# Both halves of the PE array get their block of x from one transfer, half 1 one block ahead

## The chip, the core and the metric

The kernel runs on one core of a Trainium2 chip. The core's engines work side by side, each through its own list of instructions in order: PE (matrix multiply), DVE and ACT (element-wise work), POOL (element-wise work, and it can start transfers), and SP, which in this kernel only starts transfers (DMA) between DRAM and the on-chip memory. Semaphores order the engines among each other. The metric is the device time of one execution in microseconds (us); less is better. Three runs of the kernel before took 2618.78, 2620.35 and 2619.97 us, median 2619.97.

## The reference

The input x is 2048 tokens by D = 576. What is computed, in float32:

```python
xn = layernorm(x)
qkv = (xn @ wqkv).reshape(B, S, 3, H, Dh)      # 32 heads of 18
p = softmax(q @ k.T * Dh ** -0.5)               # per head, 2048 x 2048
s = (p @ v).reshape(B, S, D) @ wo
u = xn @ w_up                                   # 576 -> 4608
g = xn @ w_gate
b = (u * g) @ w_down                            # 4608 -> 576
out = x + s * silu(b)
```

## The kernel before, in words

**Stages.** A first stage (to about 195 us in the trace) normalizes x, turns it so that D lies on partitions, makes q, k and v, and stores them in DRAM. The main stage (195 to about 2545 us) runs attention and the gated linear unit (GLU) interleaved on PE. The last stage multiplies by `wo` and writes the output.

**Two halves of PE.** In the main stage most matmuls use 64 of the 128 rows of the array, so that one on rows 0 to 63 ("half 0") and one on rows 64 to 127 ("half 1") run at the same time. PE takes its list in order; a half starts its next matmul when that matmul's turn has come and the half is free. Half 0 makes the score matmuls whose maximum DVE takes (L651) and the up projections (L756); half 1 makes the score matmuls whose exponential ACT takes (L703) and the gate projections (L756); the down projections (L807) are split over both. The product of probabilities and v (L714) takes the whole array, in 64 "visits" of 32 matmuls (64 in the trace, where each runs in two passes), two for each head.

**x for the GLU.** The 2048 tokens make four chunks (`c`) of 512. A chunk's x is cut into 9 blocks of 64 rows of D, and each value is held as a high and a low part, so `xg` (two tiles, `xg[0]` and `xg[1]`, of 9 slots each) has 18 slots per half. `x_part(b, part)` gives the tile and slot of a block's part. A projection is 27 matmuls, three for each block: `TERMS` at L746. Both halves need all 9 blocks in their own 64 rows, so before the change each half has its own transfers: `x_block(c, b, r)` copies blocks from the DRAM store `sx` into the rows of half `r`, two blocks in one transfer (block 4, which straddles the two tiles, in two small ones). SP's queue carries those of half 0, POOL's queue those of half 1 (L462). There is one buffer: block `b` of the next chunk may overwrite block `b` only after its last use, which is in the last projections of a chunk (`q == NF2 - 1 and n % 2`, L962). `x_first` fills `xg` for chunk 0 straight from the chip's memory, `x_store` writes the other chunks to `sx`.

**Units and weights.** The 4608 columns are cut in 18 parts; a unit is one chunk with one part: two up and two gate projections and 48 down matmuls on each half. In chunk 0 the weights come raw from the inputs (`g_raw`, L146: `w_up` to rows 0 to 63, `w_gate` to rows 64 to 127), are split in high and low parts by ACT and POOL, and are kept in DRAM (`swg`, `swd`); later chunks load the split weights from there (L244 into `wgu`, L283 into `wd`, 1152 KB each).

**What sets the order.** From 195 us on the order of all instructions is made by a planner at build time (`order()`, L1256). It keeps a clock for each half of PE and each engine, with fixed costs, and puts the next matmul where its inputs are due: `there` holds when blocks of x are due, `can_go` (L1189) lets a projection of a new chunk start on a block only then, `moved(start, MB)` (L1024) is its estimate for a transfer on SP's queue, `engine("POOL", ...)` the one for POOL. `stack_turn` asks for the stacks of q and k of the next head (tiles `whole` and `turning`, L319), and `max_rows` for the rows of negated maxima (L689). The planner's clock sets only the order; what runs when is set by semaphores.

The boundaries between chunks, called first, second and third below, lie near 740, 1340 and 1930 us in the trace.

Of the kernel before, what the change touches and what calls it, by code (L numbers as in the profile page):

```python
# [20 lines left out]
FT = mybir.dt.float32  # L21
# [20 lines left out]
def kernel(  # L42
# [10 lines left out]
    nc = tc.nc  # L53
    _, S, D = x.shape
# [5 lines left out]
    NCH = S // 512  # L60
# [6 lines left out]
    dram = ctx.enter_context(tc.tile_pool(name="dram", bufs=1, space=bass.MemoryType.DRAM))  # L67
# [3 lines left out]
    psum = ctx.enter_context(tc.tile_pool(name="psum", bufs=1, space=PSUM))  # L71

    sqk = dram.tile([2, 2, D, S], FT, name="sqk")
    sx = dram.tile([NCH, 9, 64, 2, 512], FT, name="sx")
    swg = dram.tile([2 * NF2, 128, 18, 128], FT, name="swg")
    swd = dram.tile([NF2, 128, 2, 2, D], FT, name="swd")
    sv = dram.tile([S, H, DH + 1], FT, name="sv")
# [67 lines left out]

    def g_raw(f):  # L146
        raw = wpool.tile([128, 9, 128], FT, name="wraw", bufs=2)
        for r, m in enumerate((w_up, w_gate)):
            nc.sync.dma_start(raw[64 * r:64 * r + 64], m[:, 128 * f:128 * f + 128].rearrange("(b p) c -> p b c", p=64))
        return raw  # L150

    def d_raw(p):
# [15 lines left out]
    clk, free, split_at = [0.0, 0.0], {"DVE": 0.0, "ACT": 0.0, "POOL": 0.0}, {}  # L168
# [7 lines left out]
    def engine(eng, start, length):  # L176
        start = max(free[eng], start)
        free[eng] = start + max(length - HIDDEN[eng], 0.03)
        return start + length
# [44 lines left out]
    def g_load(n):  # L224
        if n < 2 * NF2:
            graw[n] = g_raw(n)
# [231 lines left out]
    def x_part(b, part):  # L458
        return divmod(2 * b + part, 9)

    def x_block(c, b, r):
        queue = nc.gpsimd if r else nc.sync  # L462
        if b == 4:
            for part in range(2):
                queue.dma_start(xg[part][r:r + 64, 8 - 8 * part, :].bitcast(FT), sx[c, b, :, part, :])
        elif b in (1, 3, 6, 8):
            i, k = x_part(b - 1, 0)
            queue.dma_start(xg[i][r:r + 64, k:k + 4, :].rearrange("p (b e) s -> p b e s", b=2).bitcast(FT),
                            sx[c, b - 1:b + 1].rearrange("b p e s -> p b e s"))

    vbox, vrows, vturn = {}, [], [0]

# [48 lines left out]
    def x_store(c, ks):  # L521
        for k in ks:
            src = xcs[c][:, k, :].bitcast(FT)
            if k < 8:
                nc.sync.dma_start(sx[c, 2 * (k % 4):2 * (k % 4) + 2, :, k // 4, :].rearrange("b p s -> (b p) s"), src)
            else:
                for part in range(2):
                    nc.sync.dma_start(sx[c, 8, :, part, :], src[64 * part:64 * part + 64])

    def x_first(b, part):  # L530

        i, k = x_part(b, part)
        j, r0 = (4 * part + b // 2, 64 * (b % 2)) if b < 8 else (8, 64 * part)
        for r in (0, 64):
            nc.sync.dma_start(xg[i][r:r + 64, k, :].bitcast(FT), xcs[0][r0:r0 + 64, j, :].bitcast(FT))  # L535

    raws = {}
# [60 lines left out]
    for t in range(8, NT):  # L598
# [4 lines left out]
        if t == 11:  # L603
            xg = [xcp.tile([128, 9, 512], FR, name="xc")]
# [28 lines left out]
    with ExitStack() as mid:  # L633
# [115 lines left out]
        def gu_start(r, n):  # L749
            ready(gdone, n)  # L750
            return bank("g", 1, slots[r, "g"])
# [45 lines left out]
        def alone(u, n):  # L797
            return u == len(units) - 1 and n == 7
# [148 lines left out]
            wos[1] = wpool.tile([128, 2, D], FR, name="wos2", tag="wgu", bufs=2)  # L947
            nc.sync.dma_start(wos[1].bitcast(FT), swo[:, 8:10, :])

        passed, xdone = {}, []  # L950

        def stream(r, kind):

            def glu(n):
                c, q = units[n // 2]
                box = []
                for k in range(len(TERMS)):
                    def work(k=k):
                        if k == 0:
                            box.append(gu_start(r, n))  # L960
                        gu_op(r, n, box[0], k)
                        if q == NF2 - 1 and n % 2 and k % 3 == 2 and c < NCH - 1:  # L962
                            b = k // 3
                            x_block(c + 1, b, 64 * r)
                            if b in (1, 3, 4, 6, 8):
                                if r:
                                    at = engine("POOL", clk[r] + 0.5, 0.75 + 0.6 * (b == 4)) + 3.0
                                else:
                                    at = moved(clk[r] + 0.5, 0.285 if b == 4 else 0.57)
                                for e in (b,) if b == 4 else (b - 1, b):  # L970
                                    there["x", c + 1, e, r] = at
                        if n == 2 * len(units) - 1 and k == 13:
                            xdone.append(r)
                            if len(xdone) == 2:
                                wo_fetch()
                        if k == len(TERMS) - 1:
                            highs.append((gate_end if r else up_end)(n, box[0]))
                    end = (("DVE", 0.685) if r else ("ACT", 0.595)) if k == len(TERMS) - 1 else None
                    yield 0.231, k == 0, work, end, ("g", n, k), len(TERMS)

            def down(u, n):
                own = alone(u, n)
                key = u, n, r * own
                s, i = divmod(n, 2)
                for k in range(len(DTERMS)):
                    def work(k=k):
                        if (own or r == 0) and k == 0:
                            passed[key] = down_start(r, u)
                        down_op(r, u, s, i, passed[key], k, {"POOL": nc.gpsimd, "ACT": nc.scalar, "DVE": nc.vector}[soonest()])
                        if (own or r) and k == len(DTERMS) - 1:  # L990
                            acts.append(by_act(u, i, clk[r] + 0.33))
                            down_end(u, s, i, passed.pop(key), acts[-1])
                    end = None
                    if (own or r) and k == len(DTERMS) - 1:
                        end = (None, 0.0)
                    yield 0.132, (own or r == 0) and k == 0, work, end, ("d", u, 6 * n + k), len(DTERMS)

            if kind == "g":
                for n in range(2 * len(units)):
                    yield from glu(n)  # L1000
            else:
                for u in range(len(units)):
                    for n in range(8):
                        yield from down(u, n)
# [19 lines left out]
        def moved(start, size):  # L1024

            queue[0] = max(queue[0], start) + size / 0.24
            return queue[0] + 2.0

        due, jobs, rows_done = [], [], {}
        there, queue = {}, [0.0]  # L1030
        na = nb = 0
        part_work = len(units) * (2 * 27 * 0.231 + 4 * 12 * 0.132)
        part = part_work + (TOTAL + N + LEAD) * 0.231
# [155 lines left out]
        def can_go(r, first, ev):  # L1189

            kind, n, k = ev
            now = clk[r]
# [10 lines left out]
            c, q = units[u]  # L1203
# [10 lines left out]
                if not r and n > 0 and low_end.get(n - 1, 1e9) > now + 0.4:  # L1214
                    return False
            if c and q == 0 and n % 2 == 0:
                return there.get(("x", c, k // 3, r), 1e9) <= now
            return True

        def late(goal, r=0):  # L1220
# [117 lines left out]
    with ExitStack() as end:  # L1338
# [54 lines left out]
        for i, t in enumerate(order):  # L1393
# [17 lines left out]
            for h in range(2):  # L1411
                cs = slice(h * HALF, (h + 1) * HALF)
# [38 lines left out]
```

## Time and profile before

| what | value |
|---|---|
| median of three runs | 2619.97 us |
| the profiled execution | 2619.56 us, its span 2617.8 us (1.8 us lie around it) |
| PE busy | 2595.7 us, 99% of the span |
| DVE, ACT, POOL busy | 1782.2, 1559.3, 687.6 us |
| SP's queue (q1 in the profile) | 415.48 MB, 52.5% of the 16 DMA engines |
| POOL's queue (q0) | 15.04 MB, 1.8% |
| x from `sx`, SP | 12 transfers of 512 KB and 6 of 128 KB |
| x from `sx`, POOL | 12 transfers of 512 KB and 6 of 128 KB |

How to read it: PE counts as busy while any matmul runs, so "99%" does not say that both halves work. A row of a timeline gives the start, the length, engine, line, operation, the tile written and those read, the count of merged instructions, and in brackets the idle time of the engine ahead of it with what ended it. In a table of windows the columns are the window, its length, then for PE, PEld (weight loads), DVE, ACT and POOL the busy time and count, then the granted PE clock (1.00 is full), the busy share of the DMA engines, and GB/s.

### The profile page before, as it was taken

To read this page: it belongs to the slowest core of one execution; us is meant where nothing else is said; L and a number is where in the kernel's file an instruction comes from. 1 tells how busy PE (TensorE), PEld (TensorE's weight loads), DVE (VectorE), ACT (ScalarE), POOL (GpSimd) and SP (SyncE) were. 2 spreads that over 40 slices of the span, in tenths; PEclk is the share of its full clock that TensorE was granted. 3 is DMA by queue.
4 is the path that set the end of the run, shared out by engine and by line. 5 is a ranking of instruction groups with operands and counts; after the bars stand their busy time and mean duration, and the time that the engine had idled before them with its cause. 6 is when DMAs were issued, how large, how long until landed. Compare 5 with 4: busy or idle time off the path is not lost.

```text
span 2617.8 us, 59481 instructions
## 1 busy us (share of the span) xinstructions
PE 2595.7 (99%) x24504; PEld 2144.6 (82%) x24504; DVE 1782.2 (68%) x2951; ACT 1559.3 (60%) x3121; POOL 687.6 (26%) x721
## 2 busy tenths in 40 slices
PE   8999999999999999999999999999999999999999
PEld 7899878877778778878778887788888788877799
DVE  7208776767767777777767777677777777777136
ACT  4224666677766556666556666566666666666712
POOL 3114434444431212222121212222221222211015
PEclk9999999999999999999999999999999999999999
DMA  7799767676764445454564443453454443533366
GB/s 238 244 295 257 205 179 193 184 188 182 188 166 138 143 140 160 145 161 153 155 169 120 137 137 123 155 161 131 140 162 130 141 138 132 151 123 123 117 219 212
DMA packets 206544, 434.33 MB, mean 166 GB/s; under 512 B 82592, under 2 KB 132416, under 8 KB 176064
## 3 DMA queue, kind: packets, MB, share of 16 engines
q1 hardware_dynamic: 202096, 415.48, 52.5%
q0 software_dynamic: 4176, 15.04, 1.8%
q8 instruction: 193, 3.16, 0.5%
q14 instruction: 79, 0.65, 0.1%
HBM read 314.64 MB, written 110.56 MB: 162 GB/s over the span
## 4 chain that ended last, share of the span: by engine, by line
PE 96%; DMA 2%; SPq 1%; DVE 1%; issue 0%; ACT 0%; DVEq 0%
PE pg L756 35%; PE pg L714 17%; PE pg L807 16%; PE pa L651 11%; PE pb L703 9%; PE pg L1403 2%; PE pb L445 2%; PE pa L445 2%; PE pg L503 1%; DMA xc<-sx 1%; SPq L535 1%; DVE mx L653 0%; PE pb L1380 0%; DMA sv<-vo 0%; PE pa L703 0%; PE pg L385 0%
## 5 line engine op out<-in xcount | busy, mean ns | idle before, releaser
L653 DVE TENSOR_REDUCE mx<-pa 128x1 f32<-128x512 f32 x2016 | 1348.5, 687 | 379.1 <-PE pa L651 172.9
L705 ACT ACTIVATE pt<-pb 128x512 f32<-128x512 f32 x2003 | 1153.3, 603 | 501.1 <-PE pb L703 379.2
L756 PE MATMUL pg<-xc,wgu 64*128 64x512 f32 x7776 | 1401.9, 392 | 9.3 <-DMA xc<-sx 9.2
L756 PEld LDWEIGHTS pg<-xc,wgu 64*128 64x128 f32 x7776 | 1061.9, 186 | 55.6 <-DMA xc<-sx 6.4
L807 PE MATMUL pg<-wd,hs 64*128 64x288 f32 x6816 | 829.4, 293 | 0.0
L807 PEld LDWEIGHTS pg<-wd,hs 64*128 64x128 f32 x6816 | 775.9, 185 | 11.6 <-issue 1.7
L651 PE MATMUL pa<-whole,turning 54*128 54x512 f32 x1999 | 782.5, 398 | 0.8 <-DVE mx L653 0.7
L703 PE MATMUL pb<-whole,turning 56*128 56x512 f32 x1986 | 778.5, 398 | 0.0
L714 PE MATMUL pg<-pt,vt 128*32 128x512 f32 x4096 | 454.0, 595 | 0.0
L787 POOL TENSOR_TENSOR hs<-us,hs 128x512 fp32r<-128x512 f32 x144 | 185.9, 1291 | 1005.0 <-ACT hs L774 757.7
L651 PEld LDWEIGHTS pa<-whole,turning 54*128 54x128 f32 x1999 | 363.7, 184 | 71.5 <-issue 50.5
L703 PEld LDWEIGHTS pb<-whole,turning 56*128 56x128 f32 x1986 | 361.6, 184 | 7.7 <-ACT pt L705 0.6
L714 PEld LDWEIGHTS pg<-pt,vt 128*32 128x32 f32 x4096 | 126.6, 110 | 285.8 <-issue 281.5
L834 POOL TENSOR_TENSOR acc<-acc,st 128x288 f32<-128x288 f32 x290 | 233.3, 808 | 465.5 <-ACT st L864 297.1
L720 DVE TENSOR_TENSOR oc<-oc,pg 128x512 f32<-128x512 f32 x32 | 22.0, 688 | 220.5 <-PE pg L714 220.5
L254 POOL TENSOR_TENSOR wgu<-wraw,wgu 128x384 fp32r<-128x384 f32 x108 | 108.1, 1018 | 211.4 <-ACT wgu L253 120.0
L718 ACT ACTIVATE oc<-pg 128x512 f32<-128x512 f32 x32 | 19.1, 598 | 231.6 <-PE pg L714 231.6
L870 DVE TENSOR_TENSOR acc<-acc,pg 128x288 f32<-128x288 f32 x255 | 114.2, 449 | 41.4 <-PE pg L807 39.2
L769 DVE TENSOR_TENSOR us<-pg,us 128x512 f32<-128x512 f32 x144 | 98.5, 684 | 50.6 <-PE pg L756 31.6
L762 ACT ACTIVATE us<-pg 128x512 f32<-128x512 f32 x144 | 86.6, 602 | 69.2 <-PE pg L756 65.4
L864 ACT ACTIVATE st<-pg 128x288 f32<-128x288 f32 x290 | 119.9, 414 | 12.1 <-PE pg L807 6.0
L774 ACT ACTIVATE hs<-us 128x512 fp32r<-128x512 f32 x144 | 91.2, 634 | 26.1 <-DVE us L769 26.1
(147 smaller groups left out, 1288.7 us busy)
## 6 DMA issues: line engine op xcount, KB each, us to landing
wgu<-swg SPq DMA_DIRECT2D x102, 1152.0 KB
wd<-swd SPq DMA_DIRECT2D x50, 1152.0 KB
swg<-wgu SPq DMA_DIRECT2D x36, 1152.0 KB
whole<-sqk SPq DMA_DIRECT2D x192, 144.0 KB
turning<-sqk SPq DMA_DIRECT2D x384, 72.0 KB
swd<-wd SPq DMA_DIRECT2D x18, 1152.0 KB
sqk<-hl SPq DMA_DIRECT2D x32, 512.0 KB
wraw<-in_B_w_up_dram SPq DMA_DIRECT2D x36, 288.0 KB
```

The source lines that it names most:

```text
L254: nc.gpsimd.tensor_tensor(w[:, 9 + b:12 + b, :], raw[:, b:b + 3, :], w[:, b:b + 3, :].bitcast(FT), op=OP.subtract)
L651: nc.tensor.matmul(p, q[rows, t * 128:(t + 1) * 128], k[rows, c * 512:(c + 1) * 512], start=True, stop=True)
L653: nc.vector.tensor_reduce(mx[h][:, t, c:c + 1], p, axis=AX.X, op=OP.max)
L703: nc.tensor.matmul(p, k[rows, t * 128:(t + 1) * 128], q[rows, c * 512:(c + 1) * 512], start=True, stop=True)
L705: nc.scalar.activation(pt[t, c // 2][:, c % 2, :], p, AF.Exp, scale=scale)
L714: nc.tensor.matmul(p[32 * c:32 * c + 32, :], vt[h // 2][:, t, 6 * (h % 2):6 * (h % 2) + 32], pt[t, c // 2][:, c % 2, :], start=t == ts[0], ...
L756: nc.tensor.matmul(ps, gw[n][half[r], a, :], xg[i][half[r], e, :], start=k == 0, stop=k == len(TERMS) - 1)
L787: nc.gpsimd.tensor_tensor(hj[:, 1, :], h32, hj[:, 0, :].bitcast(FT), op=OP.subtract)
L807: op = nc.tensor.matmul(ps[:, 0:HALF], hs[u][half[r], j, a, s * 128:(s + 1) * 128], dw[u][half[r], j, e, i * HALF:(i + 1) * HALF], start=( ...
L834: nc.gpsimd.tensor_tensor(a, a, st, op=OP.add)
L864: nc.scalar.activation(st, ps[:, 0:HALF], AF.Copy)
L870: nc.vector.tensor_tensor(a, a, ps[:, 0:HALF], op=OP.add)
```

## The change

Half 1 gets the blocks of D rotated by one: its slot `b` holds block `b + 1` (slot 8 holds block 0), and the rows of `w_gate` are rotated in the same way, so that the sums are the same. Slot `b` of both halves is then the 128 rows of two consecutive blocks, and one transfer by SP fills a slot in both halves. `sx` gets a tenth block, a copy of block 0, so that slot 8 is consecutive too.

- Transfers of x per boundary: before 4 of 512 KB and 2 of 128 KB on each of SP's and POOL's queues; after 8 of 512 KB and 2 of 256 KB on SP's. POOL starts none.
- A transfer is put in the order when the slower half has passed the slot (`xhalf`), and the planner's due time `there` is one for both halves: `moved(clk + 0.5, 0.40)` for each slot.
- Two more stores of 128 KB for each of chunks 1 to 3 (`x_store`), and three loads of raw weights instead of two for each of 36 tiles (`g_raw`).

```diff
-    sx = dram.tile([NCH, 9, 64, 2, 512], FT, name="sx")
+    sx = dram.tile([NCH, 10, 64, 2, 512], FT, name="sx")
...
-        for r, m in enumerate((w_up, w_gate)):
-            nc.sync.dma_start(raw[64 * r:64 * r + 64], m[:, 128 * f:128 * f + 128].rearrange("(b p) c -> p b c", p=64))
+        cs = slice(128 * f, 128 * f + 128)
+        nc.sync.dma_start(raw[0:64], w_up[:, cs].rearrange("(b p) c -> p b c", p=64))
+        nc.sync.dma_start(raw[64:128, 0:8, :], w_gate[64:D, cs].rearrange("(b p) c -> p b c", p=64))
+        nc.sync.dma_start(raw[64:128, 8, :], w_gate[0:64, cs])
...
-    def x_block(c, b, r):
-        queue = nc.gpsimd if r else nc.sync
+    def x_block(c, b):
+        src = sx[c, b:b + 2].rearrange("b p e s -> (b p) e s")
         if b == 4:
             for part in range(2):
-                queue.dma_start(xg[part][r:r + 64, 8 - 8 * part, :].bitcast(FT), sx[c, b, :, part, :])
-        elif b in (1, 3, 6, 8):
-            i, k = x_part(b - 1, 0)
-            queue.dma_start(xg[i][r:r + 64, k:k + 4, :].rearrange("p (b e) s -> p b e s", b=2).bitcast(FT),
-                            sx[c, b - 1:b + 1].rearrange("b p e s -> p b e s"))
+                nc.sync.dma_start(xg[part][:, 8 - 8 * part, :].bitcast(FT), src[:, part, :])
+        else:
+            i, k = x_part(b, 0)
+            nc.sync.dma_start(xg[i][:, k:k + 2, :].bitcast(FT), src)
...
                 nc.sync.dma_start(sx[c, 2 * (k % 4):2 * (k % 4) + 2, :, k // 4, :].rearrange("b p s -> (b p) s"), src)
+                if k % 4 == 0:
+                    nc.sync.dma_start(sx[c, 9, :, k // 4, :], src[0:64])
...
-        j, r0 = (4 * part + b // 2, 64 * (b % 2)) if b < 8 else (8, 64 * part)
         for r in (0, 64):
+            e = (b + r // 64) % 9
+            j, r0 = (4 * part + e // 2, 64 * (e % 2)) if e < 8 else (8, 64 * part)
             nc.sync.dma_start(xg[i][r:r + 64, k, :].bitcast(FT), xcs[0][r0:r0 + 64, j, :].bitcast(FT))
...
-                            x_block(c + 1, b, 64 * r)
-                            if b in (1, 3, 4, 6, 8):
-                                if r:
-                                    at = engine("POOL", clk[r] + 0.5, 0.75 + 0.6 * (b == 4)) + 3.0
-                                else:
-                                    at = moved(clk[r] + 0.5, 0.285 if b == 4 else 0.57)
-                                for e in (b,) if b == 4 else (b - 1, b):
-                                    there["x", c + 1, e, r] = at
+                            if (c, b) in xhalf:
+                                x_block(c + 1, b)
+                                there["x", c + 1, b] = moved(clk[r] + 0.5, 0.40)
+                            xhalf.add((c, b))
...
-                return there.get(("x", c, k // 3, r), 1e9) <= now
+                return there.get(("x", c, k // 3), 1e9) <= now
```

The lines of the changed file lie two to four lower: L319 becomes L321, L468 L470, L465 L467, L651 L655, L689 L693, L703 L707, L714 L718, L756 L760, L807 L811.

The lists of all engines are the same up to the first boundary, but for SP's added loads and stores in the first stage and chunk 0. From there the planner makes another order everywhere. Three places show it.

SP's queue at the first boundary, before (`xc_1457` is `xg[0]`, `xc_1607` is `xg[1]`; `mr` are the rows of maxima, `sqk` the store of q and k, `swd` and `draw` belong to the weights of chunk 0):

```order
L689 DMA whole1_1154<-mr_10382 1x16x128 x2
L468 DMA xc_1457<-sx_72 64x2x1024
L319 DMA whole1_1154<-sqk_71 18x2048 x3
L299 DMA swd_74<-wd_10401 128x2304
L154 DMA draw_10475<-in_B_w_down_dram 128x2x576
L468 DMA xc_1457<-sx_72 64x2x1024
L465 DMA xc_1457<-sx_72 64x512
L465 DMA xc_1607<-sx_72 64x512
L468 DMA xc_1607<-sx_72 64x2x1024 x2
L319 DMA turning_1151<-sqk_71 18x1024 x6
```

And after (`xc_1466` is `xg[0]`, `xc_1616` is `xg[1]`):

```order
L693 DMA whole1_1158<-mr_10424 1x16x128 x2
L470 DMA xc_1466<-sx_72 128x1024
L321 DMA whole1_1158<-sqk_71 18x2048 x3
L301 DMA swd_74<-wd_10443 128x2304
L156 DMA draw_10517<-in_B_w_down_dram 128x2x576
L470 DMA xc_1466<-sx_72 128x1024 x3
L467 DMA xc_1466<-sx_72 128x512
L467 DMA xc_1616<-sx_72 128x512
L470 DMA xc_1616<-sx_72 128x1024
L321 DMA turning_1155<-sqk_71 18x1024 x3
L470 DMA xc_1616<-sx_72 128x1024 x3
L321 DMA turning_1155<-sqk_71 18x1024 x3
```

All of x now stands in SP's queue, the first slot alone ahead of the stacks and of two weight transfers, the others behind them, with three transfers of `turning` among them.

PE at the first boundary, before: the last matmuls ahead of the first visit of the new chunk (L714).

```order
L756 MATMUL pg<-xc,wgu 128x512
L807 MATMUL pg<-wd,hs 128x288
L703 MATMUL pb<-whole_1153,turning 128x512
L651 MATMUL pa<-whole_1153,turning 128x512
L807 MATMUL pg<-wd,hs 128x288 x12
L651 MATMUL pa<-whole_1153,turning 128x512
L756 MATMUL pg<-xc,wgu 128x512 x5
L651 MATMUL pa<-whole_1153,turning 128x512
L807 MATMUL pg<-wd,hs 128x288 x2
L714 MATMUL pg<-pt,vt 32x512 x32
```

And after:

```order
L760 MATMUL pg<-xc,wgu 128x512
L811 MATMUL pg<-wd,hs 128x288 x2
L707 MATMUL pb<-whole_1157,turning 128x512
L655 MATMUL pa<-whole_1157,turning 128x512
L811 MATMUL pg<-wd,hs 128x288 x13
L655 MATMUL pa<-whole_1157,turning 128x512 x2
L718 MATMUL pg<-pt,vt 32x512 x32
```

The five projections of the new chunk that stood ahead of the visit, half 1's first among them, now stand behind it; of the new chunk only half 0's three matmuls on slot 0 are left ahead.

PE at the last visit, before:

```order
L714 MATMUL pg<-pt,vt 32x512 x32
L807 MATMUL pg<-wd,hs 128x288
L756 MATMUL pg<-xc,wgu 128x512
L807 MATMUL pg<-wd,hs 128x288
L756 MATMUL pg<-xc,wgu 128x512
L807 MATMUL pg<-wd,hs 128x288
L756 MATMUL pg<-xc,wgu 128x512 x4
```

And after:

```order
L718 MATMUL pg<-pt,vt 32x512 x32
L811 MATMUL pg<-wd,hs 128x288 x40
L760 MATMUL pg<-xc,wgu 128x512
L811 MATMUL pg<-wd,hs 128x288 x2
L760 MATMUL pg<-xc,wgu 128x512
```

Attention ends earlier within the work and leaves more of the GLU behind it: on half 0 and half 1, before 109 and 127 projections (L756) and 189 and 192 down matmuls (L807); after 162 and 162, and 213 and 222.

More of the change, by code (lines that the diff above doesn't have):

```diff
@@ L948, in wo_rest @@
             nc.sync.dma_start(wos[1].bitcast(FT), swo[:, 8:10, :])
-        passed, xdone = {}, []
+        passed, xdone, xhalf = {}, [], set()
         def stream(r, kind):
```

## The prediction

> **What bounds it now.** First the page's totals and its row for the projections, then the list of waits on PE.
>
> ```profile
> span 2617.8 us, 59481 instructions
> PE 2595.7 (99%) x24504; PEld 2144.6 (82%) x24504; DVE 1782.2 (68%) x2951; ACT 1559.3 (60%) x3121; POOL 687.6 (26%) x721
> ...
> L756 PE MATMUL pg<-xc,wgu 64*128 64x512 f32 x7776 | 1401.9, 392 | 9.3 <-DMA xc<-sx 9.2
> ```
>
> ```profile
> PE pg L756 <- DMA xc<-sx: 9.2, 3, 4.0
> PE pg L404 <- DVE xn L353: 7.1, 2, 6.3
> ```
>
> PE bounds the kernel. What an edit can win is a wait of PE, or halves that stand idle. The wait of L404 is in the first stage; in the main stage the only one worth naming is on x, 9.2 us in three pieces. The timeline of PE shows where they lie: one at the first boundary, two at the second, none at the third.
>
> ```profile
> 754.01 1.05 PE L756 MATMUL pg<-xc,wgu 64*128 64x512 f32 x5 [3.96 <-DMA xc<-sx]
> ...
> 1360.73 0.50 PE L756 MATMUL pg<-xc,wgu 64*128 64x512 f32 x2 [2.89 <-DMA xc<-sx]
> ...
> 1365.66 0.79 PE L756 MATMUL pg<-xc,wgu 64*128 64x512 f32 x2 [2.37 <-DMA xc<-sx]
> ```
>
> The chain that ended last names the transfers, and the timelines of POOL and SP show who issued them.
>
> ```profile
> 741.72 12.15 DMA xc<-sx
> ...
> 1345.32 20.30 DMA xc<-sx
> ```
>
> ```profile
> 741.72 0.75 POOL L468 DMA_DIRECT2D xc<-sx  x1 [0.88 <-PE pg L756]
> ```
>
> ```profile
> 739.34 0.63 SPq L468 DMA_DIRECT2D xc<-sx  x1
> ```
>
> Both late transfers are POOL's: 741.72 is half 1's first pair of blocks, and 12.15 us later it is in, at 753.87, just ahead of 754.01. SP's first pair, issued 2.4 us sooner, shows as no wait. A table of windows tells what moved, and at which PE clock.
>
> ```profile
> 738.00:741.00 3.00, 3.00 (x29) 3.00 (x27) 2.59 (x5) 2.53 (x6) 2.77 (x2) 1.00 0.32 25
> 750.00:754.00 4.00, 0.05 (x1) 0.02 (x1) 0.71 (x2) 0.13 (x1) 1.37 (x2) 1.00 1.03 293
> 754.00:758.00 4.00, 3.99 (x20) 1.64 (x24) 0.69 (x1) 0.00 (x0) 0.00 (x0) 0.58 1.05 267
> 1338.00:1340.00 2.00, 2.00 (x20) 1.65 (x20) 1.88 (x3) 1.67 (x4) 1.47 (x2) 1.00 0.98 244
> 1350.00:1352.00 2.00, 2.00 (x32) 2.00 (x30) 1.82 (x5) 1.20 (x2) 0.81 (x1) 1.00 1.10 311
> 1356.00:1360.00 4.00, 1.84 (x16) 1.42 (x13) 1.38 (x2) 1.20 (x2) 0.00 (x0) 1.00 1.04 189
> 1360.00:1364.00 4.00, 2.56 (x16) 1.60 (x16) 1.38 (x2) 1.79 (x3) 0.00 (x0) 0.78 0.98 158
> 1364.00:1368.00 4.00, 2.33 (x12) 1.84 (x13) 0.69 (x1) 0.60 (x1) 0.00 (x0) 0.50 0.58 198
> ```
>
> The DMA engines are full while x loads, so 4.7 MB for a chunk take about 20 us whoever starts them; and after each wait the clock is down.
>
> **Term 1, the waits of the two boundaries: -12.7 us if they go.** The idle is 9.2 us. Lost clock is busy time by what was not granted: 3.99 x 0.42 = 1.7, 2.56 x 0.22 = 0.6, 2.33 x 0.50 = 1.2, together 3.5. The ends: 9.2 if the clock were low anyway, 12.7 if all goes. I take 12.7, since the clock stands at 1.00 ahead of each wait.
>
> [...]
>
> Do they go? That hangs on the time between the slower half's last use of a slot and the first use of the new one. I count it in the order, with these rows for the price of matmuls on two halves (L756, and scores alike: 10.92/48 = 0.23 us a pair; L807: 12.87/89.5 = 0.14) and of a visit, 7.0:
>
> ```profile
> 714.65 7.00 PE pg L714 x64
> ...
> 2519.87 10.92 PE pg L756 x96
> 2532.11 12.87 PE pg L807 x179
> ```
>
> Before, that time is 7 us for blocks 0 and 1 at the first boundary, 14 to 15 for all at the second, 22 to 23 at the third: the two that were too short are the two that waited. After, it is 7 for slot 0 and 19 to 23 for the others at the first (the visit now stands between, as the order shows); 14 for slots 0 to 4 and 22 for 5 to 8 at the second; 14 to 15 for 0 to 7 and 22 for slot 8 at the third.
>
> What a slot needs: SP's first pair moved nothing until about 2 us after its issue (25 GB/s to 741); 512 KB at 244 GB/s, the rate while SP's transfers ran alone (1338 to 1340, ahead of the shortest landing of POOL's), are 2.15; so slot 0 is in about 4.5 us after its release, and each further one 2.15 later, as one queue serves them in turn. Three transfers of `turning` (0.22 MB) add 0.9. First boundary: slot 0 needs 4.5 of 7. Behind it stand 2.2 MB of `whole`, `swd` and `draw`, 9.0 us; slot 8 is in 4.5 + 9.0 + 0.9 + 8 x 2.15 = 31.6 us after slot 0's release, and is wanted after 30.3. Second: slot 4 is in after 14.0, wanted after 17.7. Third: slot 7 in after 20.5, wanted after 21.0; the rows of maxima (L689) of the next head, now behind all ten transfers, in after about 26.5, wanted after 29.3.
>
> **Term 2, a new wait at the first boundary: +1.3 us.** That is 31.6 - 30.3. With 311 GB/s, the rate with both queues, it is 0. With 189, the row of 1356, it is about 10, and 5 more come at the third; that is a rival below. I take 244, the one row in which SP's queue ran alone.
>
> [...]
>
> **Term 3, the other order of PE: +2.6 us.** I added up, for each stretch between two visits, the half with more work. After has 9.7 us less up to the last visit and 12.3 more behind it (before 127 x 0.23 + 192 x 0.14 = 56.5, after 162 x 0.23 + 222 x 0.14 = 68.8, with unrounded prices). This counts idle halves, no waits.
>
> **Weight loads, 0 here.** In the new order ten of 50 loads of `wd` are first used 7.4 to 7.8 us after their release, in the old two. How long one takes shows late in the main stage:
>
> ```profile
> 2505.15 0.34 SPq L283 DMA_DIRECT2D wd<-swd  x1
> ```
>
> ```profile
> 2511.56 0.39 PE L807 MATMUL pg<-wd,hs 64*128 64x288 f32 x1
> ```
>
> It was in use 6.4 us after its issue, with no idle ahead of it. So 7.4 suffices where SP's queue is free: 0 as the low end, ten times about 1 us where another load shares it as the high one. I take 0, since the row has 1 us to spare.
>
> **Added issues, 0.** SP issues 36 more raw loads, 6 more stores to `sx`, and at a boundary 10 transfers of x in place of 6; POOL 6 less.
>
> ```profile
> 88.14 2.02 SPq L525 DMA_DIRECT2D sx<-xc  x3
> ...
> 114.62 0.75 SPq L149 DMA_DIRECT2D wraw<-in_B_w_gate_dram  x1
> ...
> 189.58 3.88 SPq L535 DMA_DIRECT2D xc<-xcx  x4
> ```
>
> One costs 0.6 to 0.75 us of SP. Chunk 0's loads are wanted 28 us or more after their release, so 0.75 more is covered. The start of the main stage is not covered so well: three added issues lie between 140 us and SP's last fill of `xg`, whose last four end at 193.5; they move it by about 2 us. The slot that it fills is used after 24 matmuls of half 0, 5.5 us into the stage that begins at 195.3. Cover gone, this costs up to 2. POOL's six issues (0.75 at 741.72) lay on an engine busy 26%: nothing.
>
> **Sum.** 2619.6 (the profiled execution; span 2617.8 and 1.8 around it) - 12.7 + 1.3 + 2.6 = 2610.8, so **2611 us**. The median of three, 2619.97, is 0.4 higher, within their spread. A difference of less than 0.2%, 5.2 us, can hardly be told from none here.
>
> **Rivals.**
> *Given back.* The tight `wd` loads, and stacks and rows of maxima that now queue behind x on SP, each miss by a little. Ten times 0.8 us give back the gain: 2619. For it: every load of the later chunks passes the same queue. Against: 6.4 us above, and the two such loads of before, neither followed by an idle PE.
> *Slower: one queue starves x.* SP's queue alone moves x at the 189 GB/s of 1356. Then slots come 10 us late at the first boundary and 5 at the third, with the clock's share (3.5 on 9.2) 20 us in place of 12.7: 2630. It decides from about 200 GB/s down. For it: that row, with the DMA engines full, and 158 behind it. Against: 244 with SP alone, and both slow rows fall when two queues and a load of `wd` overlap.
> *The change doesn't do what it says at the first boundary:* slot 0 misses its 7 us as POOL's pair did. A landing of 12.15, as POOL's, would leave a wait of 5 and its clock: 2617. Against: SP's own pair made it.
>
> **How the numbers follow.** Forecast, 2606 to 2615: 0.6. Given back: 0.18. Slot 0 late: 0.1, half of it still past the bound. Slower: 0.12. Faster than by 0.2% is the forecast and half of the third rival and a little of the second, 0.67; the same 0.2; slower 0.13. The range runs from 2605 (terms 2 and 3 at 0 with some idle halves less) to 2624, which takes in "given back" and leaves out the starved queue.
>
> **What would show it.** No wait of L756 on x at the second boundary, at most 2 us at the first, the clock at 1.00 through both; no x among POOL's transfers; slot 0 used without a wait; about 12 us more of PE's work behind the last visit, which starts some 20 us sooner. Wrong if PE waits on x at the third boundary, or if L807 waits for `wd`.

## The result and the profile after

The changed kernel took 2608.38 us (median of 6, 2606.43 to 2609.83), the kernel before on the same chip 2620.16 us (median of 6, 2618.65 to 2622.26). The ratio is 0.9954, 95% interval 0.9942 to 0.9967: faster, by 12 us, where 9 were forecast (2611, range 2605 to 2624).

The page of the changed kernel, its totals, the row of the projections and the two queues:

```profile
span 2606.7 us, 59535 instructions
PE 2593.6 (99%) x24504; PEld 2136.3 (82%) x24504; DVE 1774.3 (68%) x2950; ACT 1560.1 (60%) x3122; POOL 678.6 (26%) x704
...
q1 hardware_dynamic: 205264, 423.35, 53.1%
q0 software_dynamic: 2160, 7.96, 0.8%
...
L760 PE MATMUL pg<-xc,wgu 64*128 64x512 f32 x7776 | 1433.8, 392 | 1.2 <-DMA wgu<-swg 1.1
```

Its list of waits on PE:

```profile
PE pg L406 <- DVE xn L355: 6.6, 2, 6.3
PE pg L760 <- DMA wgu<-swg: 1.1, 1, 1.1
```

The 9.2 us on x are gone, at all three boundaries. What is left in the main stage is one wait of 1.1 us on a load of `wgu`, and the second profile of the same kernel (changed_again below) doesn't have it. POOL's queue moved 7.96 MB in place of 15.04: it carries no x.

The table of windows of the changed kernel, with the places that the prediction showed of before:

```profile
738.00:741.00 3.00, 3.00 (x30) 3.00 (x28) 2.59 (x5) 3.00 (x7) 2.16 (x2) 1.00 0.02 6
750.00:754.00 4.00, 4.00 (x38) 1.47 (x38) 2.08 (x4) 0.98 (x3) 2.03 (x2) 1.00 1.02 410
754.00:758.00 4.00, 4.00 (x40) 1.04 (x32) 0.00 (x0) 0.00 (x0) 0.00 (x0) 1.00 0.96 367
766.00:770.00 4.00, 4.00 (x45) 3.88 (x42) 3.63 (x7) 3.47 (x8) 0.82 (x2) 1.00 0.00 0
1346.00:1348.00 2.00, 2.00 (x31) 2.00 (x30) 1.33 (x3) 1.83 (x4) 2.00 (x3) 1.00 1.01 407
1348.00:1350.00 2.00, 2.00 (x30) 2.00 (x29) 1.32 (x2) 1.79 (x4) 1.56 (x3) 1.00 1.05 420
1356.00:1360.00 4.00, 4.00 (x40) 1.03 (x32) 0.00 (x0) 0.00 (x0) 0.00 (x0) 1.00 0.00 0
1360.00:1364.00 4.00, 4.00 (x38) 3.32 (x36) 3.25 (x5) 3.20 (x7) 0.00 (x0) 1.00 0.00 0
```

PE is full and its clock 1.00 in each. But the two columns at the end were not foreseen: in the rows at 750, 1346 and 1348, where x loads and the DMA engines are full, 407 to 420 GB/s are moved; the prediction's rows of before with full engines had 158 to 311. At the first boundary nothing moves any more from 766 on; at the second nothing from 1356 on, where before x was still on its way until 1366.

Two more rows of before's table of windows are used below, both at the second boundary:

```profile
1346.00:1348.00 2.00, 2.00 (x30) 2.00 (x28) 1.98 (x4) 1.87 (x4) 1.36 (x2) 1.00 1.06 269
1368.00:1370.00 2.00, 2.00 (x17) 0.72 (x17) 0.85 (x2) 0.00 (x0) 0.00 (x0) 0.73 0.03 14
```

The last visit and the end of the down projections behind it, from PE's timeline of before:

```profile
2482.94 7.07 PE L714 MATMUL pg<-pt,vt 128*32 128x512 f32 x64
...
2539.74 5.24 PE L807 MATMUL pg<-wdl,hs 64*128 64x288 f32 x66
```

and of the changed kernel:

```profile
2460.29 7.07 PE L718 MATMUL pg<-pt,vt 128*32 128x512 f32 x64
...
2527.79 6.43 PE L811 MATMUL pg<-wdl,hs 64*128 64x288 f32 x84
```

The last visit starts 22.6 us sooner. From its end to the end of the down projections it is 55.0 us before (2490.01 to 2544.98) and 66.9 after (2467.36 to 2534.22), 11.9 more.

### The profile page after: what moved, and what is told of

It reads as the page before. It is cut to its first block, busy times and chain, and to the rows that moved or that the text cites. A ratio compares the mean times of both kernels' runs of the same rounds, so it can differ in the third digit from the quotient of the medians.

```text
span 2606.7 us, 59535 instructions
## 1 busy us (share of the span) xinstructions
PE 2593.6 (99%) x24504; PEld 2136.3 (82%) x24504; DVE 1774.3 (68%) x2950; ACT 1560.1 (60%) x3122; POOL 678.6 (26%) x704
## 3 DMA queue, kind: packets, MB, share of 16 engines
q0 software_dynamic: 2160, 7.96, 0.8%
## 4 chain that ended last, share of the span: by engine, by line
PE 99%; DVE 0%; DMA 0%; ACT 0%; issue 0%; DVEq 0%
PE pg L760 35%; PE pg L718 17%; PE pg L811 16%; PE pa L655 11%; PE pb L707 9%; PE pb L447 2%; PE pg L1403 2%; PE pg L504 2%; PE pa L447 2%; DMA wgu<-swg 0%; PE pb L1380 0%; PE pa L707 0%; PE pg L387 0%; PE pb L655 0%; DVE mx L657 0%; DVE st L344 0%
## 5 line engine op out<-in xcount | busy, mean ns | idle before, releaser
L760 PE MATMUL pg<-xc,wgu 64*128 64x512 f32 x7776 | 1433.8, 392 | 1.2 <-DMA wgu<-swg 1.1
L760 PEld LDWEIGHTS pg<-xc,wgu 64*128 64x128 f32 x7776 | 1066.2, 186 | 52.4 <-DMA wgu<-swg 1.3
L811 PE MATMUL pg<-wd,hs 64*128 64x288 f32 x6816 | 856.9, 293 | 0.0
L811 PEld LDWEIGHTS pg<-wd,hs 64*128 64x128 f32 x6816 | 797.2, 185 | 11.4 <-issue 1.7
L655 PE MATMUL pa<-whole,turning 54*128 54x512 f32 x1999 | 782.3, 398 | 0.7 <-DVE mx L657 0.7
L707 PE MATMUL pb<-whole,turning 56*128 56x512 f32 x1994 | 780.1, 398 | 0.0
L718 PE MATMUL pg<-pt,vt 128*32 128x512 f32 x4096 | 452.7, 594 | 0.0
L655 PEld LDWEIGHTS pa<-whole,turning 54*128 54x128 f32 x1999 | 363.6, 184 | 72.4 <-issue 50.5
L707 PEld LDWEIGHTS pb<-whole,turning 56*128 56x128 f32 x1994 | 362.9, 184 | 8.3 <-ACT pt L709 0.7
L718 PEld LDWEIGHTS pg<-pt,vt 128*32 128x32 f32 x4096 | 126.5, 110 | 285.2 <-issue 278.2
```

The lines of the kernel that those rows point to most:

```text
L655: nc.tensor.matmul(p, q[rows, t * 128:(t + 1) * 128], k[rows, c * 512:(c + 1) * 512], start=True, stop=True)
L707: nc.tensor.matmul(p, k[rows, t * 128:(t + 1) * 128], q[rows, c * 512:(c + 1) * 512], start=True, stop=True)
L718: nc.tensor.matmul(p[32 * c:32 * c + 32, :], vt[h // 2][:, t, 6 * (h % 2):6 * (h % 2) + 32], pt[t, c // 2][:, c % 2, :], start=t == ts[0], ...
L760: nc.tensor.matmul(ps, gw[n][half[r], a, :], xg[i][half[r], e, :], start=k == 0, stop=k == len(TERMS) - 1)
L811: op = nc.tensor.matmul(ps[:, 0:HALF], hs[u][half[r], j, a, s * 128:(s + 1) * 128], dw[u][half[r], j, e, i * HALF:(i + 1) * HALF], start=( ...
```

## The experiments

Two questions were open. Why was x so fast, and did that, the single queue, or the other order of PE win the time? Theory F says that the form of a transfer (128 partitions or 64) sets the rate of x; its rival Q, that one queue does, which works off its transfers in turn. For the gain, theory T says that the transport removed the waits and the order cost 2.6 us (term 3); its rival O, that the order removed them. The experiments ran in three groups, each on one chip with the kernel before beside it; its medians were 2620.38 (halves_sp, parity_sp, whole_pool, old_order), 2619.84 (halves_two, before_sp, order_065, order_090) and 2619.09 us (the others), and the ratios below are to it.

### Halves, but on one queue: halves_sp

```diff
-            nc.sync.dma_start(xg[i][:, k:k + 2, :].bitcast(FT), src)
+            for r in (0, 64):
+                nc.sync.dma_start(xg[i][r:r + 64, k:k + 2, :].bitcast(FT), src[r:r + 64])
```

(and alike for block 4; the order of PE is that of the changed kernel)

> The new order and SP's queue alone, but each slot of x in two transfers of 64 partitions in place of one of 128. Theory F (the transfer over all 128 partitions sets the rate): packets of 4096 bytes take about 276 ns again, x moves at 240 to 300 GB/s, the 4.7 MB of a chunk need 16 to 20 us in place of about 12, and slot 8 of the first boundary is late by 0 to 2 us as term 2 had it: 2608 to 2612. Theory Q (one queue that works off its transfers in turn, without a second one beside it, sets the rate): packets stay near 162 ns, x at 400 GB/s or more, no wait, 2608.4 within 1.5.

Measured: 2611.09 us, ratio 0.9966 (0.9953 to 0.9978). Its windows while x loads at the first, second and third boundary:

```profile
751.00:753.00 2.00, 2.00 (x24) 0.65 (x20) 0.00 (x0) 0.00 (x0) 0.04 (x1) 1.00 1.07 172
753.00:755.00 2.00, 2.00 (x24) 0.56 (x20) 0.00 (x0) 0.00 (x0) 0.00 (x0) 1.00 1.03 229
1346.00:1348.00 2.00, 2.00 (x31) 2.00 (x30) 1.96 (x4) 1.80 (x5) 0.81 (x1) 1.00 1.04 229
1942.00:1944.00 2.00, 2.00 (x31) 2.00 (x28) 1.88 (x4) 1.80 (x4) 1.07 (x2) 1.00 1.08 237
```

and its waits on PE:

```profile
PE pa L656 <- DMA turning<-sqk: 2.4, 1, 2.4
PE pg L761 <- DMA wgu<-swg: 0.4, 1, 0.4
```

The same bytes to the same places by the same queue, only cut at partition 64: 229 GB/s against 407 in the same window of 1346 to 1348, with the DMA engines as full (1.04 against 1.01). Theory F holds and Q falls. The last two columns give an estimate of the price of 4096 bytes, the size of most packets (pieces in which a DMA engine moves a transfer; 1132 of 2168 in the changed kernel between 738 and 775 us): 16 engines busy 2.00 x 1.04 us for 458 KB or 112 packets are 0.30 us each; in the changed kernel 16 x 2.00 x 1.01 for 814 KB or 199 packets, 0.16. The packets' own times in the traces say the same: the middle one of 4096 bytes between 738 and 775 us took 285 ns in halves_sp, 159 in the changed kernel and 240 in the kernel before, whose halves came by two queues.

The time is also what the prediction gave for the changed kernel, 2611: it had priced x at 244 GB/s. That the two times agree is in part luck: a wait came, but not on slot 8, and it was 2.4 us and not 1.3: three transfers of `turning`, behind x in SP's queue, were 2.4 us late for a score.

### Which half: parity_sp and parity_again

```diff
-            nc.sync.dma_start(xg[i][:, k:k + 2, :].bitcast(FT), src)
+            for r in range(2):
+                nc.sync.dma_start(xg[i][r::2, k:k + 2, :].bitcast(FT), src[r::2])
```

> As the run with two transfers of 64 partitions for each slot on SP's queue, but one transfer takes the even partitions and one the odd ones, so that each of them reaches over all 128. If under theory F the number of partitions in a transfer counts, it is like that run (packets about 276 ns, 240 to 300 GB/s). If it counts which partitions are in flight together, it is like the changed kernel (about 162 ns, 400 GB/s, 2608.4 within 1.5). Theory Q expects the second too.

> Even and odd partitions in two transfers once more. Its first run was 1.5 us below the changed kernel's, and its profile lacks that kernel's one wait of 1.1 us on weights. If it is a faster form: 1 us or more below the changed kernel in the same call. If the two are alike, within 1 us of it.

> The changed kernel once more, beside the next three on one chip, so that differences of 1 us between them can be read: 2608.4 within 1.

Measured: 2606.87 us, ratio 0.9950 (0.9937 to 0.9962), and the second time 2607.91, 0.9956 (0.9943 to 0.9970). The changed kernel beside the second took 2607.89, 0.9956 (0.9944 to 0.9969): the two are alike, and the 1.5 us between the first run and the changed kernel were scatter. Windows of the first run:

```profile
751.00:753.00 2.00, 2.00 (x27) 0.53 (x18) 0.04 (x1) 0.00 (x0) 0.22 (x1) 1.00 1.00 402
1346.00:1348.00 2.00, 2.00 (x29) 2.00 (x28) 1.17 (x2) 1.75 (x4) 1.56 (x3) 1.00 0.81 268
```

64 partitions in a transfer are not the trouble: with every second one, 402 GB/s are moved in the first window, and where it stays at 268 the DMA engines are not full (0.81); what holds it back there is not shown. The middle packet of 4096 bytes between 738 and 775 us took 159 ns, as in the changed kernel. The number and size of the transfers are those of halves_sp, so they are not the trouble either. It counts which partitions a transfer reaches.

Why it counts is not shown in any profile here. Measured are the rates, 229 GB/s for halves against 407 in the same window, and the middle packet, 285 ns for halves against 159 with every second partition.

### All of x from POOL's queue: whole_pool

```diff
-            nc.sync.dma_start(xg[i][:, k:k + 2, :].bitcast(FT), src)
+            nc.gpsimd.dma_start(xg[i][:, k:k + 2, :].bitcast(FT), src)
```

> The changed kernel with all its transfers of x started by POOL in place of SP. Theory F: the same packets of about 162 ns and 400 GB/s, the time 2608 to 2610, since POOL may start a transfer up to 2 us late behind its element-wise work. The rival that POOL's queue itself is slow, as its first pair before the change was (12.15 us to land): packets near 276 ns, slot 0 of the first boundary late by about 5 us, 2614 to 2617.

Measured: 2611.42 us, ratio 0.9966 (0.9953 to 0.9978). A window at the second boundary:

```profile
1346.00:1348.00 2.00, 2.00 (x31) 2.00 (x29) 1.33 (x3) 1.75 (x5) 2.00 (x3) 1.00 1.03 420
```

From POOL the 128-partition form moves 420 GB/s too, so it isn't SP's queue that is fast. The time lies between the two expected ranges, and the 3 us lost are elsewhere. POOL's timeline at the first boundary and at the third:

```profile
748.57 0.53 POOL L470 DMA_DIRECT2D xc<-sx  x1 [1.87 <-DMA xc<-sx]
752.61 0.53 POOL L470 DMA_DIRECT2D xc<-sx  x1 [3.51 <-DMA xc<-sx]
...
1936.18 0.53 POOL L470 DMA_DIRECT2D xc<-sx  x1 [0.62 <-PE pg L760]
1940.07 0.53 POOL L470 DMA_DIRECT2D xc<-sx  x1 [3.35 <-DMA xc<-sx]
1940.72 1.29 POOL L791 TENSOR_TENSOR hs<-us,hs 128x512 fp32r<-128x512 f32 x1
```

and PE's at the third:

```profile
1940.12 0.67 PE L811 MATMUL pg<-wd,hs 64*128 64x288 f32 x6 [1.87 <-POOLq L815]
```

POOL stood 3.35 us ahead of a transfer until an earlier one of x had landed. A hand-over between the halves of PE (the empty instruction at L815) stands in POOL's list behind it, and PE waited 1.87 us for it. At the first boundary POOL stood 1.87 and 3.51 us, but PE waited only 0.67 us there, for slot 0. So the slow queue of the rival isn't there, and a POOL that is held in its own list is.

The trace shows for which earlier transfer POOL stands: at the first boundary the first two of ten landed at 748.04 and 752.09, and the ninth and tenth start 0.53 and 0.52 us later, at 748.57 and 752.61. In the traces of the kernel before and of the changed one POOL's transfers, 45 and 27, tell of their landing by eight semaphores, 114 to 121, given out in turn, so that a ninth has the first one's. The kernel before started six at a boundary, and its list of waits on POOL has none for a transfer of x. SP's transfers have eight semaphores too (100 to 107 in both traces), but SP has nothing else to do in this kernel.

### The new transport in the old order: old_order

```diff
                                 x_block(c + 1, b)
-                                there["x", c + 1, b] = moved(clk[r] + 0.5, 0.40)
                             xhalf.add((c, b))
+                            if b in (1, 3, 4, 6, 8):
+                                if r:
+                                    at = engine("POOL", clk[r] + 0.5, 0.75 + 0.6 * (b == 4)) + 3.0
+                                else:
+                                    at = moved(clk[r] + 0.5, 0.285 if b == 4 else 0.57)
+                                for e in (b,) if b == 4 else (b - 1, b):
+                                    there["x", c + 1, e, r] = at
...
-                return there.get(("x", c, k // 3), 1e9) <= now
+                return there.get(("x", c, k // 3, r), 1e9) <= now
```

The planner has its old costs back, and PE, DVE and ACT have the order of before, instruction for instruction.

> The new transfers, with the planner's old costs, so that PE, DVE and ACT have the order of before instruction for instruction. The new order costs 2.6 us by term 3 and widens the gap of block 1 at the first boundary from 7 to 19 us and more. Theory T (the transport alone removes the waits; the order is a cost): slots at the second boundary are in about 13.5 us after the release, wanted after 14, no wait; at the first, slot 1 stands behind 2.2 MB of other loads in SP's queue and misses its 7 us by 3 to 5; so 2619.6 - 14 + (3 to 5) = 2609 to 2611, with the tail behind the last visit back at 62 us. Theory O (the order, which moves the visit ahead of the projections, removes the waits): the wait at the first boundary stays at 4 us or more and some of the second's 5.3 us, 2613 to 2618.

Measured: 2612.86 us, ratio 0.9972 (0.9961 to 0.9982). PE's waits and the windows of the first boundary:

```profile
PE pg L760 <- DMA xc<-sx: 4.5, 1, 4.5
```

```profile
748.00:752.00 4.00, 0.39 (x5) 0.09 (x1) 0.90 (x2) 1.11 (x2) 1.26 (x1) 0.95 1.00 397
752.00:756.00 4.00, 3.09 (x20) 3.09 (x22) 1.11 (x2) 1.01 (x2) 0.09 (x1) 0.50 0.97 379
756.00:760.00 4.00, 4.00 (x31) 1.60 (x32) 1.38 (x2) 0.00 (x0) 0.72 (x1) 0.70 1.05 276
```

At the second boundary the wait is gone without the new order: the fast transport alone does that. At the first it stays: 4.5 us idle and 3.09 x 0.50 + 4.00 x 0.30 = 2.7 of clock, 7.2 together, since the second slot stands behind 2.2 MB in SP's queue and has 7 us. Both theories had a part; the time lies between their ranges. The changed kernel is 4.5 us faster than this one; by these rows and term 3 it should be 7.2 - 2.6 = 4.6.

### The new order without the new transport: halves_two

Each slot in two transfers of 64 partitions, half 0's by SP, half 1's by POOL; else the changed kernel.

```diff
-            nc.sync.dma_start(xg[i][:, k:k + 2, :].bitcast(FT), src)
+            for r, queue in ((0, nc.sync), (64, nc.gpsimd)):
+                queue.dma_start(xg[i][r:r + 64, k:k + 2, :].bitcast(FT), src[r:r + 64])
```

> The new order of PE, but each slot in two transfers of 64 partitions as before the change, half 0's by SP and half 1's by POOL. What the new order is worth without the new transfers: old_order showed the transfers without the new order, 2612.9, 4.5 above the changed kernel. Theory F: x moves at 230 to 310 GB/s as before the change; the gaps of 7 us for slot 0, and 14 us at the second boundary, are missed by 1 to 4 us each, and POOL holds its element-wise work behind transfers that wait for earlier ones, as in the run with all of x on POOL's queue: 2612 to 2617. If the order alone carried the gain, it is at 2609 or below.

Measured: 2614.02 us, ratio 0.9980 (0.9971 to 0.9989). The wait on PE, and one of its three places in POOL's timeline, 0.05 us ahead of PE's start:

```profile
PE pg L812 <- POOLq L816: 4.1, 3, 1.8
```

```profile
1344.78 0.51 POOL L471 DMA_DIRECT2D xc<-sx  x1 [2.85 <-DMA xc<-sx]
```

PE's timeline there, and the window behind it:

```profile
1344.83 0.40 PE L812 MATMUL pg<-wd,hs 64*128 64x288 f32 x2 [1.76 <-POOLq L816]
```

```profile
1346.00:1348.00 2.00, 2.00 (x20) 2.00 (x18) 1.02 (x2) 0.70 (x2) 1.03 (x2) 0.50 1.05 280
```

The time is in the expected range, but no slot was late, even at 280 GB/s, where waits of 1 to 4 us had been expected. The slots that came late before have wider gaps in the new order: blocks 0 and 1 at the first boundary, but for slot 0 itself, and those of the last two transfers, which landed at 1360.69 and 1365.62 for the waits at the second. But each transfer here also holds one slot in place of two, and what that gave was not separated. POOL again stood behind its own transfers and held PE three times, and after 1.76 us the clock was at 0.50. The order with these transfers carries a gain, 5.8 us of the change's 12. halves_sp, with the same order and all halves on SP's queue, took 2611.1: an estimate of what it is worth to leave POOL's list alone is 3 us, from runs of two groups.

### One queue in the old order: before_sp

```diff
-        queue = nc.gpsimd if r else nc.sync
+        queue = nc.sync
```

(in the kernel before)

> The kernel before with half 1's transfers on SP's queue too: one queue, but 64 partitions and the old order. Theory F: x moves at 220 to 240 GB/s as in the run with halves on SP's queue; at the first boundary half 1's first pair of blocks stands behind 2.2 MB of other loads and is 3 us or more later than on POOL's queue, so a wait of 6 to 9 us there, and the second boundary waits about as before: 2620 to 2626. Theory Q (one queue alone makes x fast): no wait at the second boundary, 2612 to 2615.

Measured: 2626.43 us, ratio 1.0027 (1.0015 to 1.0038), a loss.

```profile
PE pg L756 <- DMA xc<-sx: 14.6, 3, 8.9
```

8.9 us at the first boundary in place of 4.0, as half 1's first pair now stands behind 2.2 MB; at the second 5.7 in place of 5.3. To bring all of x by one queue is by itself a loss of 7 us. The change wins because it widens the form and the gap in the same step.

### Other orders: order_065, order_090, order_045, order_120

```diff
-                                there["x", c + 1, b] = moved(clk[r] + 0.5, 0.40)
+                                there["x", c + 1, b] = moved(clk[r] + 0.5, 0.65)
```

(and 0.90, 0.45, 1.2)

> The changed kernel with the planner's cost of a transfer of x at 0.65 in place of 0.40, which gives another order of PE. The count behind term 3 (for each stretch between two visits the half with more work) is 1.2 us less than the changed kernel's. If that count predicts the time, and no slot or weight is late: 2607.2 within 1.5. If the order's rest (waits, PSUM and DVE near the visits) outweighs it: anywhere from 2605 to 2612.

> The same with 0.90, an order whose count is 3.5 us more than the changed kernel's. If the count behind term 3 predicts the time: 2611.9 within 1.5, with the tail behind the last visit about 3 us longer (its count 69.6 against 66.8). If it doesn't, it stands at 2608 or below.

> The planner's cost at 0.45: the order differs only from the third boundary on. A finer count, in which each matmul also waits for its turn in PE's list, gives 2355.5 us for the order of before, 2358.7 for the changed one, 2367.3 for order_065 (it ran 10 us above the changed kernel, where the coarse count had said 1.2 below) and 2358.7 for this one. If the finer count holds: within 1 us of the changed kernel, its last visit about 5 us later and less behind it.

> The planner's cost at 1.2. The finer count gives 2361.7, 3.0 more than the changed order: 2611.4. But order_090, where it gave 6.8 more and the chip 17.4, has three stretches behind the first visit of a chunk in which the count is 10 us shorter than the changed kernel's and the trace only 5: no projections are left there between the scores, and DVE and ACT set the pace. This order has the same three stretches (10.9, 13.9 and 9 shorter by the count). If that pace is the cause: about 10 us more than the count, 2618 to 2623.

| order | coarse count against the changed | the same, counted again | finer count | measured | ratio to before |
|---|---|---|---|---|---|
| 0.65 | -1.2 | +6.6 | +8.6 | 2618.49 | 0.9998 (0.9989 to 1.0006) |
| 0.90 | +3.5 | +3.6 | +6.8 | 2625.77 | 1.0024 (1.0014 to 1.0033) |
| 0.45 | -0.7 | -0.5 | 0.0 | 2610.20 | 0.9966 (0.9954 to 0.9979) |
| 1.2 | +0.2 | +0.6 | +3.0 | 2634.76 | 1.0063 (1.0051 to 1.0076) |

The changed kernel took 2608.38 and, beside the last two, 2607.89. None of the four expectations held: 0.65 and 0.90 lie outside both of their branches, 0.45 is 2.3 us above the changed kernel where 1 was allowed, and 1.2 lies above its range. The coarse count is the one behind term 3. Counted again in the lists of the built kernels, by the same rule and prices, it gives the prediction's 2.6 for before against after, but +6.6 for 0.65, so the -1.2 on which that expectation rests does not come out. Even so the count fails as a forecast: it misses 0.65 by 3.5 us (by 11 with the -1.2), 0.90 by 14 and 1.2 by 26. The finer one gets 0.65 within 1.5 and 0.45 within 2.3, but misses 0.90 by 10.6 and 1.2 by 23.9. A theory that DVE and ACT set the pace where projections run out is half of it. Windows of the order of 1.2 behind the first visit of a new chunk:

```profile
762.00:766.00 4.00, 4.00 (x38) 3.50 (x35) 3.88 (x7) 4.00 (x10) 2.42 (x3) 1.00 0.21 86
766.00:770.00 4.00, 3.93 (x21) 2.24 (x18) 3.74 (x7) 3.71 (x8) 2.72 (x3) 1.00 0.34 141
770.00:774.00 4.00, 3.93 (x15) 2.27 (x15) 2.19 (x4) 2.60 (x5) 0.00 (x0) 0.63 0.78 223
774.00:778.00 4.00, 3.74 (x13) 2.77 (x14) 3.43 (x6) 2.89 (x6) 0.00 (x0) 0.50 0.17 46
778.00:782.00 4.00, 4.00 (x17) 2.11 (x17) 2.01 (x5) 2.28 (x4) 0.00 (x0) 0.50 0.00 0
```

From 766 on PE starts 21 matmuls in 4 us, not 38, while DVE and ACT are nearly full: the projections that should stand between the scores are used up. PE's list of waits shows nothing for it, since a matmul is always under way. Then the second half of the loss: the clock falls to 0.50, though this stretch's list of waits has one of 0.3 us and no other, and DVE has slack again. That was not in the expectation of 2618 to 2623. The trace's record of the granted clock has 13.65 us at 0.50 here and 6.83 behind each of the other two boundaries; half of that, 13.7 us, is an estimate of the most that it can have cost. The order of 0.90 had its clock at 1.00 throughout and still lost 17 us to the changed kernel, so the clock is not needed for a loss. How the rest of it splits over the chunks is open.

## Why the prediction was right, and where a term was off

**The forecast held:** 2611 forecast, 2608.4 measured, faster. By its own steps:

**Term 1, the waits, -12.7: right.** No wait on x, and the clock at 1.00 from the first stage to the end of the span. The last visit moved by 22.6 us, and the main stage began 0.9 later (196.20 against 195.32); with the count's 9.7 for the other order, 13.8 are left for waits and clock. That is 1.1 over the term. Of this 0.5 is known: the rows from which the term was made ended at 1368, and before's clock was still 0.73 on the mean of 1368 to 1370, 2.00 x 0.27 = 0.5 us more. The two ends, 9.2 and 12.7, were a choice between idle alone and idle with clock: the second was right, though its ground, a clock of 1.00 ahead of each wait, fails at the third: before's clock was 0.50 from 1362.24 to 1369.07, and that wait began at 1363.29.

**Term 2, a new wait of 1.3: wrong, it is 0.** It was made from 244 GB/s, "the one row in which SP's queue ran alone". That row held the rate of transfers to 64 partitions; the transfers of the change reach 128 and move 407 to 420. Slot 8 was to be in 31.6 us after slot 0's release near 741.4, at 773; nothing moved at all from 766 on. The mis-sized number is the price of a slot: 2.15 us, measured 0.52 MB at 410 GB/s = 1.28. The sum without the term is 2609.5. That one queue lands its transfers in turn, as the price per slot has it, shows in before's trace: POOL's six at the first boundary landed at 753.87, 757.02, 757.95, 758.73, 761.82 and 765.26, in the order of their issue. halves_sp, at 229 GB/s, shows what the low rate would have cost: 2.4 us of wait, though on `turning` and not on slot 8, and 2611.1.

SP alone and POOL alone move the form of the change at 407 and 420 GB/s in the window of 1346 to 1348 (changed kernel, whole_pool). For halves the count of queues does show: in the same order and window they reach 229 GB/s on one queue (halves_sp) and 280 on two (halves_two). But the form of the transfer is worth more than the second queue.

**Term 3, the order, +2.6: right in this case, and not a method.** 11.9 us more behind the last visit, where 12.3 were counted, and old_order against the changed kernel gives 4.5 where it should give 4.6. But the four other orders show that the count leaves out what can cost up to 26 us: the turns in PE's list, DVE's pace and the clock. Why it came out for before and after all the same is not shown.

**Weight loads, 0, and added issues, 0: right.** No wait of L811 on `wd`; one of 1.1 us on `wgu`, which the second profile lacks. The start of the main stage moved by 0.9, below the 2 that was the bound, and scatters by as much: 196.14 in the second profile of the changed kernel, 195.08 in order_045, whose first stage is the same.

**The rivals.** "Given back" didn't come, but its mechanism lives: in halves_sp `turning` was late behind x. "One queue starves x" had its condition met in that run for a while (172 GB/s), and cost 2.7 us there in place of 20: the low rate lasts for some windows, not for all of x. "Slot 0 late" didn't come: SP's slot 0 made its 7 us, and POOL's missed it by 0.67 in whole_pool.

**What the prediction could have seen.** In its own rows full DMA engines moved 311, 244, 189 and 158 GB/s. With the engines full the low rate came from long packets, not from an empty queue (240 ns for the middle one of 4096 bytes between 738 and 775 us, 159 after the change), and the form of the transfers is what the change alters. It was read as a limit of the queue.

## What to carry to other kernels

Price a transfer by a row of the same shape, and above all of the same partitions: the same bytes moved at 229 GB/s into 64 adjacent partitions and at 407 into 128. Where an edit re-plans the order of a saturated engine, a count of its work need not tell the time: here, with PE 99% busy, it missed by up to 26 us where the projections between the scores ran out, and four orders from one constant lay between 2610 and 2635 us. And transfers that are started by an engine that also computes can hold that engine's list: six at a boundary did not, but with ten, on eight semaphores, the ninth and tenth stood 1.87 and 3.51 us until the first and second had landed.

## What the runs showed of the hardware that was not expected

- In windows in which x loads (2 us each, two of 4), transfers of 512 KB over 128 partitions moved 367 to 420 GB/s from SP (changed kernel) and 398 to 420 from POOL (whole_pool); transfers to 64 adjacent partitions 172 to 237 on one queue (halves_sp) and 245 to 311 on two (before, halves_two); two of every second partition 260 to 420, with the DMA engines 0.76 to 1.05 busy (parity_sp, parity_again).
- POOL stood 1.87 to 3.91 us ahead of a transfer until an earlier one of x had landed, at the ninth or tenth of the ten transfers that it starts for a boundary in whole_pool and halves_two; at whole_pool's second boundary it did not. Six of them, before the change, showed no such wait (list of waits on POOL).
- The length of a wait does not tell by itself whether PE's clock falls: it was 0.50 after one of 1.76 us in halves_two, and stayed at 1.00 after one of 1.87 us in whole_pool. In the records of the granted clock of these traces every whole stretch of one value lasts a multiple of 3.41 us (at 0.50: 3.41, 6.83 or 13.65), and what was in the 3.41 us ahead of a fall differs: in halves_two all of the wait (1342.07 to 1345.48, PE busy 48%), while whole_pool's wait lies half in one such window and half in the next (border at 1939.19, PE busy 73% in each). Ahead of every fall from 1.00 PE was busy 50% of the 3.41 us or less (19 and 44% in the kernel before), but for order_120: there it was busy 92 to 96%, with only 11 to 14 matmuls. What decides a fall is not shown: in before_sp 3.41 us with 11 matmuls and PE busy 52% left the clock at 1.00.
